# Strassen for the down matmuls of two token pairs in the second MoE, with weight forms kept in DRAM

## Chip, cores and metric

One core of a Trainium2 chip runs the kernel. The metric is the device time in microseconds (us); the time given for a kernel is the median of its runs. Matrix products run on TensorE (PE), elementwise work on VectorE (DVE), ScalarE (ACT) and GpSimd (POOL), and all DMAs named here are issued in order by SyncE (SP).

## What is computed

```python
attn = np.exp(scores); attn = attn / (np.sum(attn, axis=-1, keepdims=True) + 1e-09)
x = np.matmul(attn, v)                        # 4 batches, 8 heads, 576 positions, 64 wide
x = x as [2304 tokens, 512]
xn = x / np.sqrt(np.mean(x * x, axis=-1, keepdims=True) + 1e-06) * rms_g
g = xn @ w_gate
x = silu(g) * (xn @ w_val) @ w_out            # first MoE: 512 -> 1536 -> 512
h = x @ w_in                                  # second MoE: 512 -> 2048
out = (h - np.tanh(h)) @ w_out2               #             2048 -> 512
```

## The kernel before

The 2304 tokens are cut into 6 blocks of 384. Attention runs over 20 query tiles, interleaved with the first MoE, block by block; then the second MoE runs alone. Each matmul with a weight is done in three parts: weight and activation are both split into an fp16 high and an fp16 low half, and `mm3` (L692) adds high·high, high·low and low·high, each a 128x128 by 128x384 matmul. The results of the first MoE go to DRAM (`x2d`, L734) and come back as `x2f`, 768 KB a block (`x2_load`, L1089).

The weights of the second MoE arrive as float64 words. `w2_tasks` is a list of small steps that the loops call in between the matmuls of the first MoE's last blocks and of the first block of the second MoE. A piece is loaded (512 KB, L557), decoded to fp32 by three DVE operations (`decode`, L559 to L561), squared and summed on ACT (L250), and after a power-of-two scale is known it is split in place into halves by ACT (L575) and DVE (L576). The weights then stay in SBUF in `WI` (512 -> 2048) and `W2` (2048 -> 512) to the end.

In the second MoE, blocks 0 and 1 are plain: `up2` (L1245) makes one 128-row slice of the 2048 hidden rows from 12 matmuls, 16 slices a block, and `down2` (L1260) one 128-row slice of the output from 48 matmuls, 4 a block. So a plain block has 192 matmuls up and 192 down. Blocks 2/3 and 4/5 go up as pairs by Strassen (Winograd's form): `pair_up` (L1274) makes 7 products instead of 8 for each of eight slices `s8`, each product being 2 x `mm3` = 6 matmuls, 336 matmuls a pair instead of 384. It needs sums of weight quarters (S1, S2, S4 in a tile `SF`, S3 in place of a quarter of `WI`, made by `form_tasks`, L1182 and L1181) and sums of the activations (`x2_forms`, L1126). Each product has its own PSUM bank; DVE adds them (L1302), ACT and DVE apply h − tanh h and split the result into halves (L1288 to L1291). The down half of the pairs is plain.

Order of the work: the Tile framework places each engine's instructions in one fixed list and adds the waits. An engine takes its list in order, so an instruction that waits holds up all behind it on that engine, and on SP all DMAs behind it.

## Time and profile before

| | |
|---|---|
| median of 3 runs | 1067.97 us (1066.99 to 1068.27) |
| the profiled execution, first to last instruction (span) | 1066.9 us |
| TensorE busy | 971.0 us, 91% of the span, mean granted clock 0.979 |
| VectorE busy | 680.1 us, 64% |
| ScalarE busy | 606.2 us, 57% |
| GpSimd busy | 325.6 us, 31% |
| DMA | 76.81 MB, mean 72 GB/s |

The profiled execution has no other time of its own than its span; it stands 1.1 us under the median. A matmul's row gives its start and a modelled duration of some 0.33 us, of which half lies under the next one; "idle before" is what the engine waited just before a row, and the name behind `<-` is what ended the wait. The stage windows divide the span at chosen times; PEclk is the clock that TensorE was granted as a share of full speed (1.00 is 2.4 GHz, 0.50 is 1.2 GHz).

### The profile page before, as it was taken

Reading aid. Unit: us, or ns where it says so; the run is one execution under the profiler, and the core shown is the slowest. Engines: PE = TensorE matmul, PEld = TensorE weight load, DVE = VectorE, ACT = ScalarE, POOL = GpSimd, SP = SyncE. Lnnn points to the kernel's source line nnn. Section 1 sums busy time; section 2 is a strip of 40 time slices with the busy share of each in tenths; the row PEclk is TensorE's granted clock in tenths of the full one; section 3 lists DMA queues with packets and bytes.
Section 4 is the critical chain, followed back from the end, with each engine's and each line's share of the span. In section 5 each row is a group of like instructions: output and inputs, shape, how many; then the busy total and the mean of one; then the engine's idle time right before and its main releaser. Section 6 shows DMA issues by size and latency. Waiting matters only on the chain.

```text
span 1066.9 us, 19296 instructions
## 1 busy us (share of the span) xinstructions
PE 971.0 (91%) x7471; PEld 616.9 (58%) x7472; DVE 680.1 (64%) x1472; ACT 606.2 (57%) x1172; POOL 325.6 (31%) x405
## 2 busy tenths in 40 slices
PE   1488967798899999999999899999999999999998
PEld 1377645455566666666667555655666666666664
DVE  8986998975585641674553878579792683438500
ACT  6589657776665763776766446446571462225400
POOL 5121275423462541364356112100200251015200
PEclk9986989999999999999999999999999999999999
DMA  8614524241211112210100960131102000000000
GB/s 269 257 36 108 191 72 144 65 132 38 64 27 53 25 44 74 77 28 21 54 19 11 309 233 1 46 135 68 60 1 82 8 2 16 23 23 1 8 23 30
DMA packets 49439, 76.81 MB, mean 72 GB/s; under 512 B 25891, under 2 KB 35203, under 8 KB 48835
## 3 DMA queue, kind: packets, MB, share of 16 engines
q1 hardware_dynamic: 49346, 75.58, 22.7%
q8 instruction: 58, 0.95, 0.4%
q14 instruction: 35, 0.28, 0.1%
...
## 4 chain that ended last, share of the span: by engine, by line
PE 63%; DVE 15%; DMA 9%; ACT 6%; issue 4%; POOL 2%; SPq 1%; ACTq 0%; DVEq 0%; POOLq 0%
PE m L693 11%; PE m L695 11%; PE m L694 11%; PE mm L693 7%; PE mm L695 7%; PE mm L694 7%; DVE w L560 1%; PE pv L494 1%; PE st L452 1%; PE st L453 1%; DMA wo<-wv 1%; DMA raw<-wo 1%; DMA w<-wo 1%; DVE w L559 1%; DMA qst<-qa 1%
## 5 line engine op out<-in xcount | busy, mean ns | idle before, releaser
L693 PE MATMUL mm<-xth,w 128*128 128x384 f16 x480 | 158.0, 329 | 28.2 <-DVE tm L712 20.9
L694 PE MATMUL mm<-xtl,w 128*128 128x384 f16 x480 | 157.9, 329 | 0.6 <-DMA xtl<-xl 0.6
L695 PE MATMUL mm<-xth,w 128*128 128x384 f16 x480 | 157.5, 329 | 0.1
L694 PEld LDWEIGHTS <-w 128*128 128x128 f16 x960 | 94.4, 98 | 87.1 <-issue 32.7
L693 PEld LDWEIGHTS <-w 128*128 128x128 f16 x960 | 94.9, 99 | 62.7 <-ACT w L575 3.7
L695 PEld LDWEIGHTS <-w 128*128 128x128 f16 x960 | 94.2, 98 | 63.5 <-issue 2.5
L693 PE MATMUL m<-dh,w 128*128 128x384 f16 x384 | 124.0, 326 | 0.7 <-ACT t L1271 0.7
L694 PE MATMUL m<-dl,w 128*128 128x384 f16 x384 | 124.4, 326 | 0.0
L695 PE MATMUL m<-dh,w 128*128 128x384 f16 x384 | 124.0, 326 | 0.0
L474 POOL TENSOR_TENSOR phl<-pf,phl 128x512 f16<-128x512 f32 (+2 forms) x90 | 97.8, 1094 | 40.1 <-ACT phl L467 38.7
L724 POOL TENSOR_TENSOR sl<-tm,sh 128x384 f16<-128x384 f32 x72 | 74.8, 1039 | 112.9 <-ACT sh L723 105.6
L462 POOL TENSOR_SCALAR_AFFINE_SELECT pf<-pf 128x128 f32<-128x128 f32 (+3 forms) x105 | 46.9, 449 | 175.0 <-ACT pf L460 174.7
L1263 POOL TENSOR_SCALAR io<-iso,isd 128x1 f32<-128x1 f32 x24 | 12.0, 501 | 258.8 <-ACT t L1271 258.8
L460 ACT ACTIVATE pf<-st,lnp,ilam 128x512 f32<-128x512 f32 (+2 forms) x105 | 73.0, 703 | 23.0 <-PE st L453 17.9
L1271 ACT ACTIVATE t<-m,io 128x384 f32<-128x384 f32 x24 | 13.8, 578 | 126.1 <-PE m L695 123.0
L693 PE MATMUL mm<-sh,wo 128*128 128x384 f16 x240 | 77.9, 326 | 2.3 <-DVE tm L712 2.3
L695 PE MATMUL mm<-sh,wo 128*128 128x384 f16 x240 | 78.1, 326 | 0.5 <-DVE wo L576 0.5
L694 PE MATMUL mm<-sl,wo 128*128 128x384 f16 x240 | 78.1, 326 | 0.0
L452 PE MATMUL st<-q,kl 128*128 128x128 f16 (+1 forms) x456 | 62.9, 217 | 8.6 <-DVE q L368 2.7
L1302 DVE SCALAR_TENSOR_TENSOR c<-m,sigma,c 128x768 f32<-128x768 f32 x32 | 32.5, 1015 | 57.3 <-PE m L695 55.6
L1291 POOL TENSOR_TENSOR dl<-c,dh 128x768 f16<-128x768 f32 x28 | 48.0, 1731 | 54.9 <-ACT dh L1290 54.9
L712 DVE SCALAR_TENSOR_TENSOR tm<-tm,mm 128x384 f32<-128x384 f32 x60 | 32.8, 547 | 43.9 <-ACT tm L711 41.4
...
## 6 DMA issues: line engine op xcount, KB each, us to landing
...
```

Of the source, the lines that this page charges most:

```text
L452: P.matmul(out=ps[:, o:o + w], lhsT=K2[sl][:, ks], rhs=q2_of(T)[:, h, 0:w], start=True, stop=False)
L460: A.activation(out=pf[:, 0:o], in_=ps[:, 0:o], func=ACTF.Exp, scale=bstate[b]["ilam"][:, hh:hh + 1], bias=lnp)
L462: G.affine_select(out=dg, in_=dg, pattern=[[0, len(heads)], [1, w]], compare_op=ALU.is_ge, fill=0.0, base=0, channel_multiplier=-1)
L474: G.tensor_tensor(out=u["pl"][:, 0:n], in0=u["pf"][:, 0:n], in1=u["ph"][:, 0:n], op=ALU.subtract)
L693: P.matmul(out=ps, lhsT=wh, rhs=xh, start=first, stop=False)
L694: P.matmul(out=ps, lhsT=wh, rhs=xl, start=False, stop=False)
L695: P.matmul(out=ps, lhsT=wl, rhs=xh, start=False, stop=last)
L712: V.scalar_tensor_tensor(out=t, in0=t, scalar=1.0, in1=ps, op0=ALU.add, op1=ALU.mult)
L724: moe_pend.append(lambda: G.tensor_tensor(out=SH["l"][:, f, :], in0=t, in1=SH["h"][:, f, :], op=ALU.subtract))
L1271: A.activation(out=t, in_=ps, func=ACTF.Copy, scale=io)
L1291: by.tensor_tensor(out=DL[:, s8, ds, :], in0=c[:, ds], in1=DH[:, s8, ds, :], op=ALU.subtract)
L1302: V.scalar_tensor_tensor(out=out, in0=ps, scalar=sg, in1=c0, op0=ALU.mult, op1=ALU.add)
```

## The change

The down half of the two pairs becomes Strassen as well (`pair_down`): 7 products for each of two 128-row slices `e`, each of 8 x `mm3` = 24 matmuls, so 336 matmuls a pair in place of 384. It needs the hidden activations in seven forms. Three of them (`HL`) are made in `pair_up` by `gated`; four are sums that `g_forms` makes from fp32 copies `CR`: three DVE subtractions, one ACT copy to fp16 of 4 x 384 columns, and the low halves on DVE and POOL. Two of the eight `g_forms` run inside `pair_up` (`EARLY`), six in the first three products of `pair_down`.

Both sets of weights need seven forms, which no longer fit in SBUF beside the rest. So each decoded fp32 piece is written to DRAM (`pk_d`, 32 of 256 KB), `sum_tasks` reads the pieces back (32 loads of 256 KB) while blocks 0 and 1 run, makes S1 to S4 from them on POOL and DVE, splits them (`put`), and writes all forms to DRAM as fp16 halves (`wi_d`, `wo_d`, 56 writes of 256 KB). `pair_up` then reads its weights from a ring of three buffers `wr`, one load of 128 x 7168 B (896 KB) for each `s8`, 16 in all; `pair_down` from a ring of three buffers `wd`, one load of 1 MB for each product, 14 in all. The load for a slot is issued when the last matmul that reads it is done.

PSUM: M1, M6, M7 and M4 of a slice accumulate in one bank (`ps_a`, 2 of them) and M5, M3 in another (`ps_d`, 2). Between two of those products ACT copies the partial sum out (`keep`), so the next product into that bank waits for ACT. The SBUF pool of `WI` and `W2` is closed before the pairs, and its place in the pool stack has changed.

```diff
+    pk_d = [dram.tile([128, 512], FP32, name=f"pk{i}") for i in range(32)]
+    wi_d = [dram.tile([4, 128, 7, 2, 256], FP16, name=f"wid{i}") for i in range(2)]
+    wo_d = [dram.tile([128, 2, 8, 256], FP16, name=f"wod{i}") for i in range(7)]
...
-    def mm3(ps, wh, wl, xh, xl, k, first, last):
-        P.matmul(out=ps, lhsT=wh, rhs=xh, start=first, stop=False)
-        P.matmul(out=ps, lhsT=wh, rhs=xl, start=False, stop=False)
-        P.matmul(out=ps, lhsT=wl, rhs=xh, start=False, stop=last)
+    def mm3(ps, wh, wl, xh, xl, k, first, last, free=False):
+        P.matmul(out=ps, lhsT=wh, rhs=xh, start=first, stop=False, skip_group_check=free)
+        P.matmul(out=ps, lhsT=wh, rhs=xl, start=False, stop=False, skip_group_check=free)
+        P.matmul(out=ps, lhsT=wl, rhs=xh, start=False, stop=last, skip_group_check=free)
...
+    def put(to, t, s):
+        t4 = t.rearrange("p (c w) -> p c w", c=4)
+        A.activation(out=to[:, :, 0, :], in_=t4, func=ACTF.Copy, scale=s)
+        V.scalar_tensor_tensor(out=to[:, :, 1, :], in0=t4, scalar=s, in1=to[:, :, 0, :], op0=ALU.mult, op1=ALU.subtract)
+    def keep_form(i, g, k, q, t):
+        if i == 0:
+            SY.dma_start(out=wi_d[g][:, :, q, k].rearrange("c p w -> p c w"), in_=t.rearrange("p c h w -> p c (h w)"))
+        else:
+            SY.dma_start(out=wo_d[q][:, g, 4 * k:4 * k + 4], in_=t.rearrange("p c h w -> p c (h w)"))
...
+            sq_accum(slot_f(W, n), tl[i, g % 2][:, n % 8:n % 8 + 1], junk16(raw))
+            SY.dma_start(out=pk_d[16 * i + 4 * g + k], in_=slot_f(W, n))
...
+            put(slot4(W, n), slot_f(W, n), sc[i][:, g % 2:g % 2 + 1])
+            q = {(0, 0): A11, (0, 1): A12, (1, 1): A22}.get((g // 2, k // 2))
+            if q is not None:
+                keep_form(i, g % 2, k % 2, q, slot4(W, n))
...
+    def sum_tasks(in_p, fo_p):
+        tasks = []
+        d = {}
+        def load(i, g, k):
+            for nm, gg, kk in (("a21", g + 2, k), ("a22", g + 2, k + 2), ("a11", g, k), ("a12", g, k + 2)):
+                d[nm] = in_p.tile([128, 512], FP32, name=nm, tag=nm)
+                SY.dma_start(out=d[nm], in_=pk_d[16 * i + 4 * gg + kk])
+        def form(i, g, k, q, t):
+            fo = fo_p.tile([128, 4, 2, 128], FP16, name="fo", tag="fo")
+            put(fo, t, sc[i][:, g:g + 1])
+            keep_form(i, g, k, q, fo)
+        def first(i, g, k):
+            d["t"] = in_p.tile([128, 512], FP32, name="sft", tag="sft")
+            G.tensor_tensor(out=d["t"], in0=d["a21"], in1=d["a22"], op=ALU.add)
+            G.tensor_tensor(out=d["a21"], in0=d["a11"], in1=d["a21"], op=ALU.subtract)
+        def second(i, g, k):
+            form(i, g, k, S1, d["t"])
+            form(i, g, k, S3, d["a21"])
+        def third(i, g, k):
+            V.tensor_tensor(out=d["t"], in0=d["t"], in1=d["a11"], op=ALU.subtract)
+            form(i, g, k, S2, d["t"])
+            V.tensor_tensor(out=d["a12"], in0=d["a12"], in1=d["t"], op=ALU.subtract)
+            form(i, g, k, S4, d["a12"])
+        for i in range(2):
+            for g in range(2):
+                for k in range(2):
+                    for f in (load, first, second, third):
+                        tasks.append(lambda i=i, g=g, k=k, f=f: f(i, g, k))
+        return tasks
...
-        def three(g, k):
-            t, w, v = (place(i) for i in (2 * k, 2 * k + 1, 4))
...
+    def load_up(n):
+        if n < 16:
+            wr[n] = wr_p.tile([128, 7, 2, 256], FP16, name="wr", tag="wr")
+            SY.dma_start(out=wr[n], in_=wi_d[n % 8 // 4][n % 4])
+    D_ORDER = (0, 2, 1, 3)
+    for f in range(16):
+        up2(0, f)
+        run_tasks(w2t, -(-(nt - n5) // 14))
+    run_tasks(w2t, 1000)
+    st_ws.close()
...
+    for d in D_ORDER:
+        down2(0, d)
+        run_tasks(sums, 2)
+    for f in range(16):
+        up2(1, f)
+        if f < 14:
+            run_tasks(sums, 1)
+        if f == 7:
+            x2_stat(2)
+    x2_forms(2)
+    for n in range(3):
+        load_up(n)
+    for d in D_ORDER:
+        down2(1, d)
+        run_tasks(sums, 3)
+    for st in (st_sf, st_a, st_d, st_pm):
+        st.close()
+    ps_a = pool(st_m2, "ps_a", bufs=2, space=PSUM)
+    ps_d = pool(st_m2, "ps_d", bufs=2, space=PSUM)
+    wd_p = pool(st_m2, "wd", bufs=3, side="right")
+    c_p = pool(st_m2, "cr", bufs=1)
+    t2_p = pool(st_m2, "t2", bufs=2)
+    CR = c_p.tile([128, 9, 4, TB], FP32, name="cr")
+    HL = c_p.tile([128, 8, 3, 2, TB], FP16, name="hl")
...
+        def product(ps, s8, q, form, start):
+            w = wr[8 * p + s8]
             for k in range(2):
-                h, l = wf["of"](q, g, k)
-                mm3(ps[:, 0:TB], h[:, o], l[:, o], xf[:, form, 0, k, :], xf[:, form, 1, k, :], k, k == 0, k == 1)
...
+        def keep(s8, nm):
+            t = t2_p.tile([128, TB], FP32, name=nm, tag=nm)
+            A.activation(out=t, in_=st[s8]["a"], func=ACTF.Copy, scale=sg(s8))
+            st[s8][nm] = t
+        def add(s8, i, ps, nm):
+            V.scalar_tensor_tensor(out=st[s8]["c"][:, i], in0=ps, scalar=sg(s8), in1=st[s8][nm], op0=ALU.mult, op1=ALU.add)
+        def m1(s8):
+            st[s8] = dict(a=bank(ps_a, "pa"), c=CR[:, c_at(p, s8)])
+            product(st[s8]["a"], s8, A11, B11, True)
+            keep(s8, "s1")
+        def m2(s8):
+            f = bank(ps_mm, "mm")
+            product(f, s8, A12, B21, True)
+            add(s8, 0, f, "s1")
+        def m6(s8):
+            product(st[s8]["a"], s8, S2, T2, False)
+            keep(s8, "u2")
+        def m5(s8):
+            st[s8]["d"] = bank(ps_d, "pd")
+            product(st[s8]["d"], s8, S1, T1, True)
+        def m7(s8):
+            product(st[s8]["a"], s8, S3, T3, False)
+            keep(s8, "u3")
+            add(s8, 3, st[s8]["d"], "u3")
+        def m4(s8):
+            product(st[s8]["a"], s8, A22, T4, False)
+            A.activation(out=st[s8]["c"][:, 2], in_=st[s8]["a"], func=ACTF.Copy, scale=sg(s8))
+        def m3(s8):
+            product(st[s8]["d"], s8, S4, B22, False)
+            add(s8, 1, st[s8]["d"], "u2")
...
+            A.activation(out=HL[:, s8, hs, 0, :], in_=c[:, hc], func=ACTF.Copy)
+            (V if s8 == 7 else G).tensor_tensor(out=HL[:, s8, hs, 1, :], in0=c[:, hc], in1=HL[:, s8, hs, 0, :], op=ALU.subtract)
...
         for s8 in range(8):
-            product(m1, "11", B11, s8)
-            A.activation(out=s1[:, 0], in_=m1[:, 0:TB], func=ACTF.Copy, scale=sg)
-            product(m26[:, 0], "12", B21, s8)
-            product(m26[:, 1], "S2", T2, s8)
-            add(c[:, 0:2], m26[:, :, 0:TB], s1.to_broadcast([128, 2, TB]))
-            product(m7, "S3", T3, s8)
-            add(c[:, 2], m7[:, 0:TB], c[:, 1])
-            product(m5, "S1", T1, s8)
-            add(c[:, 1:4:2], m5[:, 0:TB].unsqueeze(1).to_broadcast([128, 2, TB]), c[:, 1:3])
-            product(m34[:, 0], "S4", B22, s8)
-            product(m34[:, 1], "22", T4, s8)
-            rest(c, s8, 0, 3, V if s8 == 7 else G)
-            add(c[:, 1:3], m34[:, :, 0:TB], c[:, 1:3])
-            rest(c, s8, 1, 1, V if s8 == 7 else G)
+            m6(s8)
+            m5(s8)
+            if s8 < 7:
+                m1(s8 + 1)
+            m7(s8)
+            gated(s8, slice(0, 4, 3), slice(0, 2), slice(0, 4, 3))
+            if s8 < 7:
+                m2(s8 + 1)
+            m4(s8)
+            m3(s8)
+            gated(s8, slice(1, 3), 2, 2)
+            load_up(8 * p + s8 + 3)
+            if s8 in EARLY:
+                g_forms(p, EARLY.index(s8))
+            if j == 2 and s8 == 4:
+                x2_stat(4)
+    EARLY = (3, 5)
...
+    def c_at(p, s8):
+        return (9 - p + s8) % 9
+    def g_form(p, s8):
+        return CR[:, (8 - p + s8) % 9].rearrange("p a t -> p (a t)").bitcast(FP16).rearrange("p (f l t) -> p f l t", f=4, l=2)
+    def g_forms(p, s8):
+        c = CR[:, c_at(p, s8)]
+        V.tensor_tensor(out=c[:, 0:2], in0=c[:, 1:4:2], in1=c[:, 0:2], op=ALU.subtract)
+        V.tensor_tensor(out=c[:, 3], in0=c[:, 3], in1=c[:, 0], op=ALU.subtract)
+        V.tensor_tensor(out=c[:, 2], in0=c[:, 2], in1=c[:, 3], op=ALU.subtract)
+        t = g_form(p, s8)
+        A.activation(out=t[:, :, 0, :], in_=c, func=ACTF.Copy)
+        for e, fs in ((V, slice(0, 2)), (G, slice(2, 4))):
+            e.tensor_tensor(out=t[:, fs, 1, :], in0=c[:, fs], in1=t[:, fs, 0, :], op=ALU.subtract)
+    DOWN = [(A11, "h", 0), (A12, "h", 2), (S4, "h", 1), (S2, "t", 3), (S3, "t", 1), (S1, "t", 0), (A22, "t", 2)]
+    def load_down(n):
+        if n < 14:
+            wd[n] = wd_p.tile([128, 2, 8, 256], FP16, name="wd", tag="wd")
+            SY.dma_start(out=wd[n], in_=wo_d[DOWN[n % 7][0]])
...
+        for i, (q, kind, f) in enumerate(DOWN):
+            w = wd[7 * p + i]
+            for e in range(2):
+                s = st[e]
+                if q == A11:
+                    s["a"] = bank(ps_a, "pa")
+                if q == S1:
+                    s["d"] = bank(ps_d, "pd")
+                ps = s["a"] if q in (A11, S2, S3, A22) else s["d"] if q == S1 else bank(ps_mm, "mm")
+                for s8 in range(8):
+                    v = HL[:, s8, f] if kind == "h" else g_form(p, s8)[:, f]
+                    mm3(ps, w[:, e, s8, 0:128], w[:, e, s8, 128:256], v[:, 0, :], v[:, 1, :], s8, s8 == 0 and q not in (S2, S3, A22), s8 == 7, True)
+                if q == A11:
+                    s["s1"] = keep(ps, e, "s1")
+                elif q == A12:
+                    total(j, e, ps, s["s1"])
+                elif q == S4:
+                    s["m3"] = keep(ps, e, "m3")
+                elif q == S2:
+                    s["u2"] = keep(ps, e, "u2")
+                    V.tensor_tensor(out=s["m3"], in0=s["m3"], in1=s["u2"], op=ALU.add)
+                elif q == S3:
+                    s["u3"] = keep(ps, e, "u3")
+                elif q == S1:
+                    total(j + 1, e, ps, s["m3"])
+                    total(j + 1, e + 2, ps, s["u3"])
+                else:
+                    t = out_tile()
+                    A.activation(out=t, in_=ps, func=ACTF.Copy, scale=io[:, e:e + 1])
+                    send(j, e + 2, t)
+            if i < 3:
+                with newest() if i == 0 else ExitStack():
+                    for s8 in range(2 + 2 * i, 4 + 2 * i):
+                        g_forms(p, s8)
+            load_down(7 * p + i + 3)
+            if i == 3 and j == 2:
+                with newest():
+                    x2_forms(4)
+    run_tasks(sums, 1000)
+    for n in range(3):
+        load_down(n)
+    for j in (2, 4):
+        if j == 2:
+            x2_load(4)
+            x2_load(5)
+        pair_up(j)
+        pair_down(j)
```

The change moves instructions at three places. First, **SP around the first loads of the second MoE's weights** (`w<-win`, while block 4 of the first MoE runs); `xth`/`xtl` are the transposed activations of the first MoE's last block. Before:

```order
L557 DMA w2_8286<-win 128x1024 x11
L547 DMA_TRANSPOSE xth_7255<-xh_8015 128x4x128
L557 DMA w2_8286<-win 128x1024
L548 DMA_TRANSPOSE xtl_7256<-xl_8016 128x4x128
L557 DMA w2_8286<-win 128x1024 x2
```

Now:

```order
L1116 DMA x2f_8793<-x2d_115 128x1536
L537 DMA_TRANSPOSE xth_7296<-xh_8056 128x4x128
L538 DMA_TRANSPOSE xtl_7297<-xl_8057 128x4x128
L547 DMA w2_8339<-win 128x1024 x8
L1042 DMA pk0_116<-wi_8338 128x512
L547 DMA w2_8339<-win 128x1024
L1042 DMA pk1_117<-wi_8338 128x512
```

The loads now stand behind the two transposes, and from the ninth on each stands behind a write of a decoded piece.

Second, **DVE in the same stretch**. `wi<-w2` rows are decodes (three a piece), `tm<-tm,mm` rows are the first MoE's own gate and value work, which frees PSUM banks for PE. Before:

```order
L561 SCALAR_TENSOR_TENSOR wi_8285<-w2_8286,wi_8285 128x512
L544 SCALAR_TENSOR_TENSOR ss_8014<-ss_8014 128x1
L712 SCALAR_TENSOR_TENSOR tm_8060<-tm_8060,mm_8046 128x384
L559 TENSOR_SCALAR wi_8285<-w2_8286 128x512
L543 TENSOR_SCALAR ss_8014<-ss_8014 128x1
L722 SCALAR_TENSOR_TENSOR tm_8060<-tm_8060,mm_8063 128x384
L559 TENSOR_SCALAR wi_8285<-w2_8286 128x512
```

Now:

```order
L702 SCALAR_TENSOR_TENSOR tm_8101<-tm_8101,mm_8087 128x384
L536 SCALAR_TENSOR_TENSOR xl_8057<-x_7881,ss_8055,xh_8056 128x512
L712 SCALAR_TENSOR_TENSOR tm_8101<-tm_8101,mm_8104 128x384
L702 SCALAR_TENSOR_TENSOR tm_8133<-tm_8133,mm_8119 128x384
L712 SCALAR_TENSOR_TENSOR tm_8133<-tm_8133,mm_8136 128x384
L549 TENSOR_SCALAR wi_8338<-w2_8339 128x512
L550 SCALAR_TENSOR_TENSOR wi_8338<-w2_8339,wi_8338 128x512
L551 SCALAR_TENSOR_TENSOR wi_8338<-w2_8339,wi_8338 128x512
```

All of block 4's own DVE work now comes ahead of the first decode; the decodes follow in one run of 15 pieces before block 5's first `tm` row.

Third, **PE in `pair_up` around the first reuse of a ring slot**. `pa` and `pd` are the accumulating banks, `wr` the ring's buffers; the rows are the last matmul of M3 of slice 0, the first of the four products behind it (6 matmuls each), and the first matmul of M1 of slice 3. Now:

```order
L685 MATMUL pd_10635<-xf_9173,wr_10278 128x384
L683 MATMUL pa_10642<-xf_9173,wr_10280 128x384
...
L683 MATMUL pd_10702<-xf_9173,wr_10280 128x384
...
L683 MATMUL pa_10709<-xf_9173,wr_10282 128x384
...
L683 MATMUL pd_10769<-xf_9173,wr_10282 128x384
...
L683 MATMUL pa_10776<-xf_9173,wr_10692 128x384
```

SP at the same place. Now:

```order
L1398 DMA wd_10604<-wod6_156 128x4096
L1247 DMA wr_10692<-wid0_148 128x3584
L1247 DMA wr_10759<-wid1_149 128x3584
L1247 DMA wr_10826<-wid1_149 128x3584
L1247 DMA wr_10893<-wid1_149 128x3584
```

Buffer `wr_10692` takes the slot of `wr_10278`, so its load can start only behind the first of these PE rows, and the last PE row waits for it: four products, 24 matmuls, lie between. The slices run in pairs, so the same pattern comes back at slices 5 and 7, and three times in the second pair: six places. At the other slices more than ten products lie between.

## Rows read from the trace of the kernel before

**Rows 1.** Windows by stage: start:end us, length, busy us (xcount) by engine, PEclk, DMA share, GB/s.

```profile
600.00:640.00 40.00, 39.42 (x242) 23.63 (x242) 33.58 (x64) 19.70 (x51) 5.56 (x3) 1.00 0.81 259
715.00:730.00 15.00, 12.20 (x74) 7.11 (x73) 14.28 (x30) 10.31 (x23) 0.00 (x0) 1.00 0.41 134
730.00:760.00 30.00, 30.00 (x187) 18.21 (x186) 29.76 (x62) 19.64 (x34) 5.75 (x2) 1.00 0.21 66
840.00:880.00 40.00, 40.00 (x248) 24.09 (x247) 35.45 (x38) 25.32 (x33) 21.27 (x12) 1.00 0.00 1
```

**Rows 2.** Timeline, second MoE's first and last matmul and what follows: start us, us, instruction.

```profile
699.02 0.33 PE L693 MATMUL m<-x2f,wi 128*128 128x384 f16 x1
...
1063.15 0.33 PE L695 MATMUL m<-dh,w 128*128 128x384 f16 x1
...
1063.56 0.58 ACT L1271 ACTIVATE t<-m,io 128x384 f32<-128x384 f32 x1 [8.10 <-PE m L695]
```

**Rows 3.** Waits of PE from 560 us on: us in total, times, longest.

```profile
PE mm L693 <- DVE tm L712: 2.9, 2, 1.4
PE m L693 <- DVE tm L712: 2.8, 2, 2.4
PE m L693 <- DVE t L1256: 2.5, 3, 1.2
PE m L693 <- ACT t L1271: 0.7, 1, 0.7
```

**Rows 4.** Timeline of PE: three rows behind a wait, [idle before <-releaser].

```profile
594.46 0.32 PE L693 MATMUL mm<-xth,w 128*128 128x384 f16 x1 [1.44 <-DVE tm L712]
...
599.96 0.32 PE L693 MATMUL mm<-sh,wo 128*128 128x384 f16 x1 [1.44 <-DVE tm L712]
...
642.20 0.32 PE L693 MATMUL m<-xth,w 128*128 128x384 f16 x1 [2.42 <-DVE tm L712]
```

**Rows 5.** Windows of 1 us behind the longest of these waits.

```profile
643.00:644.00 1.00, 1.00 (x5) 0.46 (x3) 1.00 (x4) 1.00 (x4) 0.00 (x0) 0.50 0.00 0
646.00:647.00 1.00, 1.00 (x7) 0.57 (x6) 0.74 (x1) 0.59 (x2) 0.56 (x1) 0.83 0.09 16
```

**Rows 6.** Timeline of DVE: the first decode of the second MoE's weights.

```profile
591.94 0.43 DVE L559 TENSOR_SCALAR wi<-w 128x512 int32<-128x512 int32 x1 [1.71 <-DMA w<-win]
```

**Rows 7.** Groups of DVE from 560 to 720 us: busy us, mean ns of one.

```profile
L560 DVE SCALAR_TENSOR_TENSOR wi<-w,wi 128x512 int32<-128x512 int32 x16 | 10.9, 685 | 0.0
```

**Rows 8.** Groups from 730 us to the end, shapes apart.

```profile
L1291 POOL TENSOR_TENSOR dl<-c,dh 128x768 f16<-128x768 f32 x28 | 48.0, 1731 | 54.9 <-ACT dh L1290 54.9
L1288 ACT ACTIVATE ta<-c,isd 128x768 f32<-128x768 f32 x32 | 29.8, 932 | 29.9 <-DVE c L1302 29.9
L1290 ACT ACTIVATE dh<-c 128x768 f16<-128x768 f32 x32 | 26.8, 840 | 8.7 <-DVE c L1289 8.6
L1305 ACT ACTIVATE c<-mm,sigma 128x384 f32<-128x384 f32 x16 | 9.2, 576 | 7.1 <-PE mm L695 7.1
L1133 ACT ACTIVATE xf<-x2f 128x1536 f16<-128x1536 f32 x4 | 5.9, 1479 | 3.9 <-DMA x2f<-x2d 3.2 <-DVE sf L1182 0.7
```

**Rows 9.** Timeline of SP: issue of one 768 KB load.

```profile
734.39 0.33 SPq L1091 DMA_DIRECT2D x2f<-x2d  x1
```

**Rows 10.** Windows over that load's data.

```profile
736.50:737.00 0.50, 0.50 (x6) 0.30 (x4) 0.50 (x3) 0.50 (x2) 0.00 (x0) 1.00 0.99 393
737.50:738.00 0.50, 0.50 (x5) 0.31 (x4) 0.50 (x2) 0.08 (x1) 0.00 (x0) 1.00 0.74 307
738.00:738.50 0.50, 0.50 (x5) 0.30 (x4) 0.50 (x2) 0.00 (x0) 0.00 (x0) 1.00 0.01 0
```

**Rows 11.** Timeline of SP and ACT: a 768 KB load between two writes, and its reader.

```profile
753.93 0.34 SPq L1272 DMA_DIRECT2D out<-t  x1
754.32 0.43 SPq L1091 DMA_DIRECT2D x2f<-x2d  x1
...
760.59 1.48 ACT L1133 ACTIVATE xf<-x2f 128x1536 f16<-128x1536 f32 x1 [3.24 <-DMA x2f<-x2d]
```

More of the change, by code (lines that the diff above doesn't have):

```diff
@@ L105, in tile_forget_attention_moe_moe2 @@
     wide = [None]
-    half = []
-    pairs = [bool(0)]
-    def mm_pair():
-        half.clear()
-        return wide[0].tile([128, 2, 512], FP32, name="m2", tag="m2", bufs=2)
     def mm_tile():
-        if wide[0] is not None and not pairs[0]:
+        if wide[0] is not None:
             return wide[0].tile([128, 512], FP32, name="m2", tag="m2", bufs=4)[:, 0:TB]
-        if pairs[0]:
-            if not half:
-                pair = mm_pair()
-                half.extend(pair[:, i, 0:TB] for i in range(2))
-            return half.pop(0)
         return ps_mm.tile([128, 512], FP32, name="mm", tag="mm")[:, 0:TB]
@@ new lines, in tile_forget_attention_moe_moe2, with p2 @@
+    sc = [small(const, [128, 2], FP32, f"sc2{i}") for i in range(2)]
+    simin, sig = small(const, [128, 1], FP32, "simin"), small(const, [128, 2], FP32, "sigma")
+    def p2(src, e, sg):
+        V.tensor_scalar(out=e, in0=src.bitcast(I32), scalar1=24, scalar2=None, op0=ALU.logical_shift_right)
+        V.tensor_scalar(out=e, in0=e, scalar1=37.0, scalar2=50.0, op0=ALU.max, op1=ALU.add)
+        V.tensor_scalar(out=e, in0=e, scalar1=23, scalar2=None, op0=ALU.logical_shift_left)
+        V.reciprocal(out=sg, in_=e.bitcast(FP32))
@@ new lines, in w2_tasks @@
+        for i in range(2):
+            for g in range(2):
+                for gg in (g, g + 2):
+                    for k in range(4):
+                        tasks.append(lambda i=i, gg=gg, k=k: piece(i, gg, k))
+                tasks.append(lambda i=i, g=g: chain(i, g))
+                for gg in (g, g + 2):
+                    for k in range(4):
+                        tasks.append(lambda i=i, gg=gg, k=k: conv(i, gg, k))
+            if i == 0:
+                tasks.append(last)
+                n_in = len(tasks)
@@ L1086, in tile_forget_attention_moe_moe2 @@
     x2s = {}
-    XF = [None]
     def x2_load(j):
@@ L1353, in tile_forget_attention_moe_moe2 @@
+    run_tasks(sums, 1000)
[7 more added lines that the diff above has]
+        pair_down(j)
+    for st in (st_m2, st_w2):
         st.close()
```

292 lines of the change are left out of this document (104 added, 188 removed).

## Prediction

> **What bounds the kernel now.** I read the windows by stage first, then the waits of PE in the second half, then the timeline around each wait. From 730 us to the end PE is busy in every stage, as in the stretches at 730 and at 840 us, at full clock [rows 1]. So the second MoE is bound by the number of its matmuls, and a matmul less is worth its spacing. That comes from the first and the last matmul of the second MoE, 699.02 and 1063.15 us [rows 2]. Between them lie 4 x 192 plain up, 2 x 336 Strassen up and 4 x 192 plain down, 2208 in all, and some 3.8 us of waits (the two rows for the second MoE give 3.2 [rows 3], a wait too short for a row of its own here another 0.6). (1063.15 − 699.02 − 3.8) / 2207 = 0.163 us. The half-overlapped 0.33 us of a row is not the cost.
>
> PE's other stalls from 560 us on lie in the end of the first MoE: 2.9 and 2.8 us behind DVE's `tm`, two each [rows 3]. DVE is the busier helper there: 33.58 of 40 us from 600 to 640, and 14.28 of 15 from 715 to 730, where PE has 12.20 [rows 1]. It decodes the second MoE's weights in the same list.
>
> **The change, part by part.** All sums are against the profiled span of 1066.9 us; the median of the runs is 1.1 us above it, which I add at the end.
>
> *Removed matmuls.* The down of a pair falls from 384 to 336; 2 x 48 = 96 x 0.163 = **−15.6 us**. All of them lie on the path.
>
> *First decodes.* Before, the first decode sits in DVE's list ahead of block 4's `tm`, and waits for its load until 591.94 after 1.71 us idle [rows 6]. PE then stands 1.44 us twice, at 594.46 and 599.96, for `tm` [rows 4]. Now all of block 4's `tm` rows come ahead of the first decode. **−2.9 us**; bounds −2.9 and 0.
>
> *Later decodes.* The price is that decoding starts some 8 us later (the loads stand behind two transposes), near 600 us. A decode row takes 0.685 us [rows 7]; with its two companions a piece takes about 1.5, so the 15 pieces ahead of block 5's first `tm` end near 624 us. PE has 144 down matmuls of block 4 and block 5's first ones in between, and needs that bank near 628. So I expect no new wait there, and little of the old ones in block 5: 2.8 us in waits [rows 3], of which 2.42 stand at 642.20 [rows 4], and behind that one the granted clock is half, 0.50 (1.2 GHz), for three windows of 1 us and 0.83 in a fourth [rows 5], which loses 3 x 0.5 + 0.17 = 1.7 us. At stake are 4.5 us. DVE is still full, so I take **−3 us**; bounds −4.5 and +2 (15 decodes end 6 us late).
>
> *Plain up of block 0.* The wait for DVE's `t` is 2.5 us [rows 3]. Fewer pieces fall into it, but the writes and form splits add some. **−2 us**; bounds −3 and +2.
>
> *Forming the sums.* 8 rounds, each four loads, two POOL operations, two DVE subtractions, four splits on ACT and DVE and four writes, in down 0, up 1 and down 1: 576 matmuls or 94 us, 11.7 us a round, and 7.8 in up 1, where a round takes four slices of 12 matmuls. On SP the loads stand in one line behind the writes and the outputs. PE's list in down 1 mixes slices of the output, so a late step is seldom waited for. **+2 us** for this and for the handover of pools to the pairs; bounds 0 and 8.
>
> *The rings in `pair_up`.* This is the change's new wait. Between the last matmul that reads a buffer and the first that needs its reload lie 24 matmuls, 24 x 0.163 = 3.9 us, at six places; elsewhere ten products or more. No load of 896 KB into a busy kernel is in the trace. Lower bound: a lone 768 KB load is issued at 734.39 [rows 9], runs at up to 393 GB/s, and its data has ended within the window that closes at 738.00 [rows 10], 3.6 us; scaled by size only the data part of 2 us grows, by 0.3, so 3.9: no wait. Upper bound: the load issued at 754.32 beside two writes of 192 KB lets its reader start at 760.59, 6.27 us [rows 11]; 6.6 for 896 KB, 2.7 us late, six times 16. The ring's loads have SP and the DMA engines nearly alone, as the lone one has, so I take 4.6 us with the release and landing, 0.7 late at each, **+4 us**; bounds 0 and 16, and more if the clock falls in the waits.
>
> A rule bears on this. The Trainium skill, "DMA: Bandwidth & Descriptors", section Bandwidth, lists 6.15 us for a 1 MB load; an estimate from it for 896 KB is 5.4 us, six waits of 1.5 us, and the sum would be 5 us higher. The trace is at odds with it: its lone 768 KB load is done in 3.6 us from issue to the last data [rows 9, 10].
>
> *ACT in `pair_up`.* The copies of partial sums sit between products of one bank. For each slice ACT does four copies of 384 columns at 0.576, two tanh at 0.932, copies of 768 (0.840) and 384 columns (0.576) [rows 8]: 5.6 us; PE has 42 matmuls, 6.8 us. Two slices with one early form add 1.48 (the 1536-column row): 12.7 of 13.7. ACT fits, without much slack; **+2 us** for short waits, bounds 0 and 6.
>
> *Forms in `pair_down`.* Six forms, each ACT 1.48 and then POOL 1.73 [rows 8], 19.3 us end to end, while the first three products give PE 3 x 48 x 0.163 = 23.5 us. The cover is there; without it the first S2 product waits up to 4 us a pair. **0**; bounds 0 and 8. The `wd` loads have 7.8 us or more of matmuls each. **0**.
>
> *End.* As before: the last matmul, an ACT copy at 1063.56 [rows 2], a write. **0**.
>
> Sum: −15.6 − 2.9 − 3 − 2 + 2 + 4 + 2 = −15.5, a span of 1051.4, against the median **1052.5 us**. A measurement of this kernel can tell about 0.2%, 2.1 us, from no change; so faster means under 1065.8, slower above 1070.1.
>
> **Rivals.**
>
> *The rings come late (slower).* If a reload takes 7.5 us instead of 4.6, the wait is 3.6 at six places, 22 us; and if the clock falls behind each, as it did behind 2.42 us [rows 5], 1.7 more each, 10 us. The sum without the ring is 1048.5; the time would be 1070 to 1080. It decides at a wait of 3.2 us a place (or 1.5 with the clock). For it: the load that took 6.27 us to its reader. Against it: that one ran beside two others. I give a middle case, waits of 1.5 to 2.5 us, 1058 to 1064, 0.12, and the slow end 0.09.
>
> *Everything is hidden.* The ring waits for nothing, and the stalls of block 5 and of up 0 all go: −15.6 − 2.9 − 4.5 − 2.5 = 1041.4 span; with a little left over 1043 to 1047. For it: PE has been kept full through every stretch from 730 us on. Chance 0.15.
>
> *The helpers bind between 600 and 800 us.* DVE was at 29.76 of 30 from 730 us [rows 1], and now it also splits sums and waits in line for SP's loads; block 5 and block 0 stall as before and block 1 stalls for 5 us more: 1057 to 1062. For it: DVE's share; against it: POOL, with nothing to do from 715 to 730 us and 5.75 of 30 after that [rows 1], takes half of the sums' additions. Chance 0.15.
>
> *The change does less than it says.* The forms of `pair_down` come late at both pairs, 8 us each: 1066 to 1070, no change. PE would stand before the first S2 product. Chance 0.05.
>
> **How the numbers follow.** The forecast itself (1047 to 1057) gets 0.44, the hidden case 0.15, helpers 0.15, middle ring 0.12, late forms 0.05, slow ring 0.09. Range 1044 to 1062: it leaves out the late forms, the slow ring, the lower part of the hidden case and the upper part of the middle ring. Faster 0.44 + 0.15 + 0.15 + 0.12 = 0.86; same 0.05; slower 0.09.
>
> **What would show it.** PE has 96 matmuls fewer. No wait of PE for `tm` between 590 and 605 us, and less than 2 us in block 5. In each `pair_up`, PE waits for a DMA into `wr` at three places, 0.5 to 1 us each, and nowhere else for a DMA. Waits of PE for ACT copies sum to about 2 us. None for POOL in `pair_down`. The granted clock stays 1.00 from 700 us on. The prediction is wrong if PE waits for `wr` over 2 us a place, if the clock is at half in `pair_up`, or if the stretch from the last product of block 1 to the first of `pair_up` has a hole of over 3 us.

## The result and the profile after

The changed kernel takes 1073.99 us (median of 5 runs, 1072.48 to 1077.85) against 1068.2 us before: ratio 1.0053, 95% interval 1.0037 to 1.007. It is slower by half a percent, where 1052.5 us and faster were forecast; the time lies outside the range. The profiled execution spans 1074.3 us, 7.4 us more than before; its time of 1075.98 us stands 2.0 us above the median.

The page, part 1 (busy us, share of the span and instructions of each engine):

```profile
PE 964.1 (90%) x7372; PEld 607.1 (57%) x7372; DVE 726.7 (68%) x1518; ACT 660.7 (62%) x1256; POOL 370.8 (35%) x421
```

TensorE has 99 records fewer (96 are the removed matmuls, and the scales of the weights need 4 records fewer; a record is missing here or there), and yet a lower share than the 91% of before, while all four other engines have more to do. The waits of PE from 560 us on, total us, times and longest, to be held against [rows 3]:

```profile
PE mm L683 <- DVE t L1413: 4.0, 2, 2.0
PE pa L683 <- DMA wr<-wid: 3.3, 5, 0.8
PE m L683 <- DVE t L1226: 3.0, 4, 1.4
PE mm L684 <- DVE xf L1170: 2.9, 1, 2.9
PE pa L683 <- ACT u L1304: 2.8, 3, 1.3
PE mm L683 <- DVE tm L702: 1.8, 1, 1.8
PE pd L683 <- DVE cr L1308: 1.7, 2, 0.9
PE m L683 <- DVE x2e L121: 1.5, 1, 1.5
PE m L683 <- ACT t L1239: 1.5, 1, 1.5
PE pa L684 <- POOL cr L1391: 1.1, 2, 0.6
PE mm L683 <- DVE cr L1308: 1.1, 1, 1.1
PE pa L683 <- ACT cr L1389: 0.5, 1, 0.5
PE m L683 <- DVE tm L702: 0.3, 1, 0.3
```

Before, this list had the four kinds of [rows 3] and one more of 0.6 us, 9.5 us together; now it has thirteen and 25.5. The windows by stage tell where they lie (columns as in [rows 1]):

```profile
760.00:780.00 20.00, 16.63 (x101) 9.82 (x100) 12.15 (x18) 9.91 (x18) 4.55 (x5) 1.00 0.77 262
780.00:800.00 20.00, 14.37 (x82) 7.93 (x80) 19.33 (x37) 15.34 (x26) 4.17 (x3) 0.96 0.63 197
900.00:920.00 20.00, 17.98 (x111) 10.74 (x110) 14.50 (x21) 8.21 (x11) 6.61 (x3) 1.00 0.54 193
1020.00:1040.00 20.00, 17.98 (x101) 10.27 (x100) 13.80 (x20) 7.81 (x9) 6.66 (x4) 0.91 0.36 125
```

Before, PE was busy all through both stretches from 730 us on in [rows 1], and its one wait there was 0.72 us at 1055.51 us. The first and the last matmul of the second MoE:

```profile
695.36 0.33 PE L683 MATMUL m<-x2f,wi 128*128 128x384 f16 x1
...
1070.53 0.33 PE L685 MATMUL pa<-cr,wd 128*128 128x384 f16 x1
```

The second MoE's part, from its first matmul to the end of the span, is 1074.3 − 695.36 = 378.9 us; before it was 1066.9 − 699.02 = 367.9 [rows 2]. So it grew by 11.0 us although 15.6 us of matmuls left it. In what follows "part" means this stretch, and it is used to compare profiles: its start lies anywhere between 690.2 and 697.3 us in the profiles of the kernels below, whose first 560 us hold the same program.

A wait costs more than the idle time in its row: behind 2.02 us idle the matmuls start 911.27 − 908.92 = 2.35 us apart instead of 0.16 (rows below), 0.17 more than the idle time. For a list of waits I add 0.16 each.

### The profile page after: what moved, and what is told of

It reads as the page before. It is cut to its first block, busy times and chain, and to the rows that moved or that the text cites. A ratio compares the mean times of both kernels' runs of the same rounds, so it can differ in the third digit from the quotient of the medians.

```text
span 1074.3 us, 19602 instructions
## 1 busy us (share of the span) xinstructions
PE 964.1 (90%) x7372; PEld 607.1 (57%) x7372; DVE 726.7 (68%) x1518; ACT 660.7 (62%) x1256; POOL 370.8 (35%) x421
## 4 chain that ended last, share of the span: by engine, by line
PE 44%; DVE 23%; DMA 11%; issue 8%; ACT 7%; POOL 5%; SPq 1%; POOLq 0%; ACTq 0%; DVEq 0%
PE mm L683 8%; PE mm L685 7%; PE mm L684 7%; POOL cr L1391 3%; PE m L683 2%; PE m L685 2%; PE m L684 2%; PE pa L684 2%; PE pa L683 2%; PE pa L685 2%; PE pv L484 2%; PE st L442 1%; DMA wr<-wid 1%; DVE w L550 1%; PE st L443 1%
## 5 line engine op out<-in xcount | busy, mean ns | idle before, releaser
L683 PE MATMUL mm<-xth,w 128*128 128x384 f16 x480 | 160.4, 334 | 25.2 <-DVE tm L702 16.5
L685 PE MATMUL mm<-xth,w 128*128 128x384 f16 x480 | 159.6, 334 | 0.0
L464 POOL TENSOR_TENSOR phl<-pf,phl 128x512 f16<-128x512 f32 (+2 forms) x90 | 94.8, 1061 | 40.4 <-ACT phl L457 38.0
L684 PEld LDWEIGHTS <-w 128*128 128x128 f16 x704 | 69.7, 99 | 65.2 <-issue 27.9
L685 PEld LDWEIGHTS <-w 128*128 128x128 f16 x704 | 69.7, 99 | 47.7 <-issue 3.7
L683 PEld LDWEIGHTS <-w 128*128 128x128 f16 x704 | 70.0, 99 | 46.9 <-ACT w L565 3.7
L1347 POOL TENSOR_TENSOR hl<-cr,hl 128x768 f16<-128x768 f32 (+1 forms) x28 | 41.9, 1501 | 105.4 <-ACT hl L1346 105.4
L443 PE MATMUL st<-qc,kc 128*128 128x128 f16 (+1 forms) x456 | 59.1, 216 | 0.6 <-DMA qc<-rt 0.6
L457 ACT ACTIVATE phl<-pf 128x512 f16<-128x512 f32 (+2 forms) x90 | 49.4, 558 | 11.9 <-POOL pf L452 6.2
L713 ACT ACTIVATE sh<-tm 128x384 f16<-128x384 f32 x72 | 37.1, 517 | 29.0 <-DVE tm L712 28.7
L1391 POOL TENSOR_TENSOR cr<-cr 128x768 f16<-128x768 f32 x16 | 37.7, 2354 | 45.2 <-ACT cr L1389 45.2
L442 PEld LDWEIGHTS <-kl 128*128 128x128 f16 x480 | 45.1, 103 | 13.4 <-DVE kl L288 7.8
L486 PE MATMUL pv<-vt,phl 128*128 128x65 f16 (+1 forms) x360 | 49.7, 196 | 2.2 <-ACT phl L457 1.5
```

The costliest lines, as they stand in the source:

```text
L442: P.matmul(out=ps[:, o:o + w], lhsT=K2[sl][:, ks], rhs=q2_of(T)[:, h, 0:w], start=True, stop=False)
L443: P.matmul(out=ps[:, o:o + w], lhsT=KC[sl][:, ks], rhs=qc_of(T)[:, h, 0:w], start=False, stop=True)
L457: A.activation(out=ph[:, 0:o], in_=pf[:, 0:o], func=ACTF.Copy)
L464: G.tensor_tensor(out=u["pl"][:, 0:n], in0=u["pf"][:, 0:n], in1=u["ph"][:, 0:n], op=ALU.subtract)
L486: P.matmul(out=ps[0:w, o:o + 65], lhsT=u["ph"][:, cs], rhs=vs[:, 64:129], start=(c == 0), stop=False)
L683: P.matmul(out=ps, lhsT=wh, rhs=xh, start=first, stop=False, skip_group_check=free)
```

## The experiments

### What holds up PE between 760 and 800 us

Seven waits lie there, 8.9 us idle, 10.0 with the 0.16 each, and the half clock behind the last of them, 1.7 us more. Ahead of them stands one long gap on ACT. SP's issues, then ACT and PE in the changed kernel:

```profile
753.91 0.84 SPq L1247 DMA_DIRECT2D wr<-wid  x2
754.85 0.40 SPq L1024 DMA_DIRECT2D wid<-fo  x1
755.98 0.99 SPq L1247 DMA_DIRECT2D wr<-wid  x1
...
756.20 0.56 ACT L1239 ACTIVATE t<-m,io 128x384 f32<-128x384 f32 x1
764.28 0.72 ACT L1019 ACTIVATE fo<-a,sc 128x512 f16<-128x512 f32 x1 [7.52 <-DMA wid<-fo]
...
765.52 0.32 PE L683 MATMUL m<-xf,wi 128*128 128x384 f16 x1 [1.48 <-ACT t L1239]
```

The scheduler has put the first three loads of the ring, 2.75 MB, ahead of or between the form writes, at 753.91 and 755.98 us. ACT's next form copy waits 7.52 us for a form buffer, that is for a write which stands in the same DMA queues; behind it in ACT's list stand the output copy that PE waits for and all tanh rows of up 1. That was my first theory (A); the rival (B) was that the work on the sums holds up up 1 however the loads come.

**e1_late_wr** spreads the three loads (`after_sp` holds a load behind SP's newest instruction):

```diff
+        if f in (9, 12, 15):
+            with after_sp():
+                load_up((f - 9) // 3)
     x2_forms(2)
-    for n in range(3):
-        load_up(n)
```

> The three first loads of the ring of pair_up come one by one behind later rows of SP (the first behind four more rounds' rows), instead of all three at 753.9 to 757.0 us. Theory A (the burst): 2.75 MB put into the DMA queues at once made the write of a form buffer last 9 us, so ACT stood 7.52 us for that buffer and everything of up 1 came late. Then ACT's longest wait for a form write falls under 2 us, PE's waits between 760 and 800 us (8.9 us in seven) fall under 4 us, the half clock behind 798 us goes, and the time falls by 6 to 10 us to 1064 to 1068. Rival B (DVE and ACT simply have too much work in up 1 and down 1): the hole of ACT goes, but PE waits over 7 us in that stretch all the same, and the time stays within 3 us of 1074.

Measured: 1076.69 us (ratio to before 1.0085, 1.006 to 1.011), part 381.2 us. ACT's waits for form buffers and sums from 740 to 800 us:

```profile
ACT fo L1019 <- POOL sft L1092: 5.3, 3, 2.8
ACT fo L1019 <- DMA wid<-fo: 2.2, 2, 1.7
```

The gap is gone (1.7 us at most for the write), and PE still waits 10.4 us in six places between 760 and 794 us. A falls: the burst makes the gap, but the gap is not what costs the time.

**e2_fo6** (`"fo", bufs=6` for `bufs=3`) leaves the burst and gives ACT room.

> Six buffers for the forms in sum_tasks instead of three; the three ring loads stay where they are. Theory A: the write in the queue behind the burst is still slow, but ACT has three more buffers to go on with, so its 7.52 us wait falls under 3 us and PE's waits between 760 and 800 us under 5 us; time 1065 to 1070. Rival B (too much work): PE's waits there stay above 7 us. Rival C (the loads of the fp32 pieces stand behind the burst too, so POOL and DVE starve): ACT's wait for the form write goes but one of similar length for POOL's sum comes in its place, and the time stays above 1071.

Measured: 1073.44 us (1.0041, 1.0026 to 1.0055), part 379.1. The gap changed its name, as rival C said:

```profile
ACT fo L1019 <- POOL sft L1092: 11.6, 4, 8.7
```

The longest of these is 8.7 us: the loads of the fp32 pieces stand behind the burst as well. PE's waits there are 7.1 us in four.

**e7_no_sums** takes the sums out (`sums = []`, and `conv` writes the quarters' halves in the places of S1 to S4).

> The weight sums S1 to S4 are not formed: sum_tasks is left out, and the four forms are written to DRAM as copies of the quarters' halves, so the output is not the reference's. The 56 form writes, the rings, the pairs and all their matmuls stay as they are. It measures what forming the sums costs PE. Theory B (the sum steps in the in-order lists of ACT and DVE hold up the tanh work that frees PE's banks): PE's waits between 745 and 800 us, 8.9 us in seven in the changed kernel with a half clock behind the last, fall under 2 us, and the span falls by about 10 us to 1062 to 1066. Theory A (the burst of ring loads alone): the same burst now meets form writes made in block 0, ACT waits for nothing in up 1, and the result would be the same; so this run gives the size, and the late-load run has already told the two apart. Rival D (the waits there come from x2_stat and x2_forms, which are still in): 5 us or more of waits stay.

Measured in one run: span 1062.6, part 366.7 us, 12.2 less than the changed kernel; between 690 and 830 us PE has no wait at all. x2_stat and x2_forms are still in, so rival D falls. This is the size of the largest cost: forming the sums beside blocks 0 and 1 costs PE 12 us.

**e8_spread** (8 steps in up 1 instead of 14, up to 16 in down 1):

```diff
-        if f < 14:
+        if f % 2 == 0:
             run_tasks(sums, 1)
...
-        run_tasks(sums, 3)
+        run_tasks(sums, 4)
```

> Up 1 runs 8 steps of sum_tasks instead of 14 and down 1 up to 16 instead of 12: what only pair_down needs is formed later. Theory B: the PE waits of 8.9 us between 760 and 800 us fall to 3 to 6 us, since fewer steps stand in ACT's and DVE's lists ahead of the tanh rows; time 1066 to 1071. If the sums' steps in up 1 did not matter (Theory A alone), the wait of ACT behind the burst stays at 5 to 8 us and the time within 2 us of 1074.

Measured: 1074.67 us (1.0071, 1.0049 to 1.0093), part 379.5; the same seven waits, 9.6 us. It tells nothing about B: ACT's list is the same row for row, since the scheduler fills its list by what it reckons to be ready, not by where the program calls the steps. In letters (f a form copy of the sums, O an output copy, T a tanh of up 1; all other rows left out), for the changed kernel, this one, and the next:

```
changed    ffffOfffOffffOfOTTfTfTfTfTfTfTfTfTfTfTfTfTfTfTffffOOffOO
e8_spread  ffffOfffOffffOfOTTfTfTfTfTfTfTfTfTfTfTfTfTfTfTffffOOffOO
e10_paced  ffffOfffOfOOTTTTTffTTfTfTTTTTffTTTffOffOfffOfffffOffffff
```

**e10_paced** fixes the places: each step of the sums is held behind the newest row of ACT and DVE, two rounds in up 1, four in down 1.

```diff
-        if f < 14:
-            run_tasks(sums, 1)
+        if f % 2 == 0:
+            with newest():
+                run_tasks(sums, 1)
...
-        run_tasks(sums, 3)
+        with newest():
+            run_tasks(sums, 4)
```

> The steps of sum_tasks are held behind the newest work of ScalarE and VectorE, so that their place in those lists is fixed: two rounds in up 1 (one step for every second slice), four in down 1; six form buffers, and the three ring loads one by one behind SP's newest row. Leaving the sums out took PE's waits between 745 and 800 us from 8.9 us to none and the second MoE's part of the span from 378.9 to 366.7 us, so forming them costs 12 us. Theory B (the sum steps stand in the lists ahead of the tanh rows and wait there for GpSimd and the loads): PE's waits in up 1 fall under 3 us, and the second MoE's part of the span falls to 369 to 374 us. Rival (the work of the sums is too much for the engines wherever it stands): the waits move to down 1 and the start of pair_up, and the part stays above 376 us.

Measured: 1081.34 us (1.0124, 1.011 to 1.0138), part 387.2. Up 1 has no wait left, as B said, but the start of `pair_up` pays more, as the rival said (waits of PE from 690 to 860 us, then POOL's first row of three rounds):

```profile
PE pa L683 <- ACT cr L1347: 7.1, 1, 7.1
PE pa L683 <- ACT t L1239: 4.6, 1, 4.6
```

```profile
813.54 1.26 POOL L1092 TENSOR_TENSOR sft<-a,a 128x512 f32<-128x512 f32 x1 [5.78 <-DMA a<-pk]
823.08 1.26 POOL L1092 TENSOR_TENSOR sft<-a,a 128x512 f32<-128x512 f32 x1 [6.93 <-DMA a<-pk]
835.83 1.26 POOL L1092 TENSOR_TENSOR sft<-a,a 128x512 f32<-128x512 f32 x1 [10.14 <-DMA a<-pk]
```

The round that starts at 813.54 us takes 9.5 us. The rows point to its one set of piece buffers: a load of the next round goes out at 818.56 us, 0.5 us behind a DVE row that read a piece of this one (it ends at 818.09), and POOL starts 4.5 us behind that load. The round behind it takes 12.8 us, and POOL's wait of 10.1 us has a second cause: two loads of `wd`, 1 MB each, were issued ahead of three of that round's pieces, at 824.78 and 826.63 us. The long wait of PE, 7.1 us, is a handover: ACT's row of `cr`, which ends it, starts at 843.95 us, after 2.17 us idle for a form write of the last round (`wod<-fo`). Both theories were half of it: the steps hold up the tanh rows where they stand ahead of them, and eight rounds of some ten us in line are too long to be moved out of the way.

### The ring in `pair_up`

```profile
846.90 2.27 SPq L1247 DMA_DIRECT2D wr<-wid  x2
...
850.45 0.33 PE L685 MATMUL pd<-xf,wr 128*128 128x384 f16 x1
851.54 0.34 PE L683 MATMUL pa<-xf,wr 128*128 128x384 f16 x1 [0.77 <-DMA wr<-wid]
```

The rows are SP's issue of the reload and PE's matmuls around the wait. From the issue at 846.90 to the first matmul with the new weights at 851.54 it is 4.64 us; 4.6 were forecast, five waits of 0.58 to 0.77 us in place of six of 0.7. **e4_ring4** gives the ring a fourth buffer (`bufs=4`, loads four ahead).

> Four buffers in the ring of pair_up instead of three. Theory A: the five waits of PE for the ring (0.58 to 0.77 us each, 3.3 us, with the refill of the pipe behind each 4.1 us) are the reload that takes 4.6 us where 3.9 are covered; with a fourth buffer no reload is waited for, and 3 to 4 us go. The burst ahead of pair_up is one load longer (3.67 MB), so ACT's wait for a form write grows by up to 2.4 us and takes 0 to 3 us of it back: 1070 to 1074. Rival (the DMA engines are too slow for the ring in itself): waits for the ring stay, fewer but longer.

Measured: 1071.14 us (1.0027, 1.0015 to 1.004), part 375.8, 3.1 us less, as theory A said; no wait for `wr` is left.

### `pair_down`

DVE, then PE, at the start of the first `pair_down`:

```profile
906.13 2.68 DVE L1385 TENSOR_TENSOR cr<-cr 128x768 f32<-128x768 f32 x3
908.74 1.48 DVE L1386 TENSOR_TENSOR cr<-cr 128x384 f32<-128x384 f32 x3
910.61 0.60 DVE L1413 SCALAR_TENSOR_TENSOR t<-mm,io,s 128x384 f32<-128x384 f32 x1
...
908.92 0.33 PE L685 MATMUL mm<-hl,wd 128*128 128x384 f16 x1
911.27 0.32 PE L683 MATMUL mm<-hl,wd 128*128 128x384 f16 x1 [2.02 <-DVE t L1413]
```

PE's second product there needs a bank of `ps_mm` that DVE empties at 910.61 us (L1413); ahead of it in DVE's list stand the subtractions of six `g_forms`, from 906.13 us on. **e3_s4_bank** gives the S4 product a bank of `ps_d`, which is free there.

> In pair_down the S4 product takes the banks of the pool ps_d, which are free there, instead of ps_mm. Theory A: PE's 2.02 us in each pair_down is a wait for a bank of ps_mm, which VectorE frees late because the subtractions of g_forms stand ahead of it in its list. Then both waits go, with the half clock behind the second, and about 2 x 2.2 + 1.7 = 6 us at most; but the forms, a chain of ACT and POOL that takes 4.0 us each, then set when S2, S3 and S1 start, so that 2 to 4 us of it come back there: net gain 2 to 4 us, 1070 to 1072. Rival (the wait only covers the wait for the forms): PE waits 2 us a pair more on POOL and ACT behind it, and the time does not change.

Measured: 1074.86 us (1.0051, 1.0035 to 1.0068), part 377.4, 1.5 us less. The time has not changed, as the rival said: the waits of 2.02 us are gone, but PE waits 1.65 us for POOL in each pair, and 0.2 to 0.7 us at five places behind it: the forms are next. They come every 4.0 us (ACT's copies at 915.08 and 919.09; ACT, DVE and POOL in turn):

```profile
915.08 1.48 ACT L1389 ACTIVATE cr<-cr 128x1536 f16<-128x1536 f32 x1 [2.81 <-POOL cr L1391]
...
916.59 0.96 DVE L1391 TENSOR_TENSOR cr<-cr 128x768 f16<-128x768 f32 x1 [3.05 <-ACT cr L1389]
...
916.64 2.42 POOL L1391 TENSOR_TENSOR cr<-cr 128x768 f16<-128x768 f32 x1 [1.59 <-ACT cr L1389]
...
919.09 1.48 ACT L1389 ACTIVATE cr<-cr 128x1536 f16<-128x1536 f32 x1 [2.06 <-POOL cr L1391]
```

DVE and POOL start on two halves of the same work at the same time, DVE takes 0.96 and POOL 2.42 us. **e9_low_s4** puts both halves on DVE, with S4 in `ps_d`:

```diff
-        for e, fs in ((V, slice(0, 2)), (G, slice(2, 4))):
+        for e, fs in ((V, slice(0, 2)), (V, slice(2, 4))):
```

> S4 in the free banks as before, and the low halves of all four forms on VectorE instead of two on GpSimd. A row of 768 columns takes VectorE 0.96 us; beside it GpSimd's took 2.41, where it took 1.65 alone. Theory: the two engines hold each other up, and the chain of a form (ACT 1.48, then the slower of the two low halves 2.41, 4.0 in all) falls to ACT 1.48 and 1.92, 3.5 in all. Then the waits of PE for GpSimd in pair_down (1.65 and 0.69 us) go, and the time falls by 3 to 6 us to 1068 to 1071. Rival: the bound is ACT waiting for the buffer that the form before leaves, whoever makes the halves; then PE's waits only change the engine they name and the time stays within 2 us of 1074.

Measured: 1067.9 us, the same as before (0.9997, 0.9978 to 1.0016), 6 us under the changed kernel; part 373.5, from the slowest of its ten runs. ACT's copies now stand 3.46 us apart (913.71 and 917.17 us), near the 3.5 of the theory. A new wait came instead: PE stands 1.85 and 1.60 us for a load of `wd`, once in each pair. The low halves on DVE without the free bank were not run, so the 6 us belong to the two edits together. The two groups, POOL's of the changed kernel and then DVE's of this one, 880 us to the end:

```profile
L1391 POOL TENSOR_TENSOR cr<-cr 128x768 f16<-128x768 f32 x14 | 33.2, 2372 | 40.7 <-ACT cr L1389 40.7
```

```profile
L1391 DVE TENSOR_TENSOR cr<-cr 128x768 f16<-128x768 f32 x28 | 25.6, 955 | 17.1 <-ACT cr L1389 16.9
```

Twice as many rows on DVE take 25.6 us, less than POOL's half alone did.

### The early forms in `pair_up`

ACT, then PE:

```profile
857.64 1.49 ACT L1389 ACTIVATE cr<-cr 128x1536 f16<-128x1536 f32 x1 [0.97 <-DVE cr L1387]
859.03 1.03 ACT L1304 ACTIVATE u<-pa,sigma 128x384 f32<-128x384 f32 x2
...
859.64 0.32 PE L683 MATMUL pa<-xf,wr 128*128 128x384 f16 x1 [1.10 <-ACT u L1304]
```

The form's copy of 1536 columns waits 0.97 us for DVE's subtractions and takes 1.49; the copy of a partial sum that PE waits for stands behind it. **e6_no_early** (`EARLY = ()`, eight forms in `pair_down`):

> None of the eight forms of a pair is made inside pair_up; pair_down makes all eight. Theory: in pair_up the forms' ACT copy of 1536 columns, which waits for VectorE's subtractions, stands in ACT's list ahead of the copies of partial sums, so PE waits 1.1, 0.9 and 0.4 us in the first pair and 1.3 and 0.9 in the second. Without it those five waits go (4.5 us, 5.3 with the refills), and pair_down gets two forms of 4.0 us more to wait for, 4 to 8 us a pair: span 1077 to 1085. Rival (x2_stat or the matmuls' own pace causes them): the waits for ACT and VectorE in pair_up stay.

Measured in one run: span 1085.7, part 392.8 us. The five waits in `pair_up` are gone, and `pair_down` lost some 9.5 us a pair, more than the 4 to 8 expected. The early forms are worth their waits.

### Together

**e11_ring4_low_s4** is e4 and e9 in one.

> Four ring buffers in pair_up, S4 in the free banks and all low halves of the forms on VectorE, the sums as in the changed kernel. The effects lie at different places, so they should add: 3 us for the ring, 6 for the last two together, 9 in all: 1064 to 1067, against 1074 of the changed kernel and 1067.5 to 1068.4 of the kernel before. If VectorE becomes the bound in pair_up (its waits for cr rose where the ring no longer waited), the gain is 6 or less and the time 1067 to 1070.

Measured: 1060.66 us (1057.97 to 1062.38), ratio to before 0.9929 (0.9916 to 0.9943): faster than both kernels, and 13 us under the changed one where 9 were expected. The part is 366.9, 12.0 us under the changed kernel's, where e4 and e9 had 3.1 and 5.4. PE's 3.4 us of waits for `wd`, which were in e9, are gone here, and they are about the rest; why the load comes in time here was not tried. What PE still waits for, the three largest from 690 us on:

```profile
PE m L683 <- DVE t L1226: 3.0, 4, 1.4
PE mm L684 <- DVE xf L1170: 2.5, 1, 2.5
PE m L683 <- ACT t L1239: 1.8, 1, 1.8
```

**e12_all** adds the paced sums, **e13_paced12** the same with three rounds in up 1 (`if f < 12`, and 3 steps for each output slice in down 1).

> The version before this one with the paced sums as well (three form buffers). If theory B holds and the effects add, 9 us for pair_up and pair_down and 5 to 10 us for the sums: 1055 to 1063, faster than the kernel before by 0.5 to 1.2%. If the sums' work is too much wherever it stands, 1064 to 1070.

> As the version with everything, but three rounds of the sums in up 1 (one step behind each of the first 12 slices) and up to three in down 1. With two rounds up 1 had no wait of PE at all and the start of pair_up 13 to 17 us of waits, since four rounds did not fit beside down 1; with the order left to the scheduler up 1 had 7 to 9 us and the start of pair_up 1. If a round costs some 8 us of its chain wherever it stands, three in 31 us of up 1 and two or three in 31 us of down 1 fit nearly, and the waits in both places together fall under 6 us: part of the second MoE 360 to 365 us, time 1053 to 1060. Rival (ScalarE's and VectorE's tanh work leaves no room for a third round in up 1): waits of 6 us or more come back there and the time is 1060 to 1066.

Measured: 1066.85 us (0.9993, 0.9982 to 1.0004) and 1063.17 us (0.9939, 0.992 to 0.9957). Neither beats e11, and both times fell into the range of the rival, though in e13 up 1 waits only 3.9 us, and the start of `pair_up` 5.4. Pacing moves the rounds' cost, it does not remove it. A second set of buffers for the pieces was not tried, so that the one set of buffers makes a round this long is read from the rows and not shown by a run.

## Why the prediction was wrong, point by point

The forecast span was 1051.4 us, the measured one 1074.3.

- *Removed matmuls, −15.6*: right. They are gone, and e7 shows a part below that of before in spite of 15 us of other waits.
- *First and later decodes, −5.9*: the waits of [rows 4] and the half clock of [rows 5] are gone, but a new one came. The rows of ACT, then PE:

```profile
593.86 1.48 ACT L1142 ACTIVATE x2f<-x2f 128x1536 f16<-128x1536 f32 x1 [1.77 <-DMA x2f<-x2d]
...
596.62 0.32 PE L683 MATMUL mm<-xth,w 128*128 128x384 f16 x1 [1.77 <-DVE tm L702]
```
  The square of the first `x2f`, moved up in ACT's list, waits 1.77 us for its load, which SP now issues ahead of the transposes; `tm` and PE wait with it. I had listed that load and weighed only what stood behind it on SP. The part starts 3.7 us earlier in the profile, but that understates the gain, since this execution was late before the change began. PE's first matmul behind the last row of attention, before and then now:
```profile
587.50 0.32 PE L693 MATMUL mm<-xth,w 128*128 128x384 f16 x1
```
```profile
589.32 0.32 PE L683 MATMUL mm<-xth,w 128*128 128x384 f16 x1
```
  From there to the second MoE it is 111.5 us before and 106.0 now, so the term came to 5.5 us, 0.4 short, and 1.8 us of the difference between the two spans lie ahead of it.
- *Plain up of block 0, −2*: all of it went, and with it a wait of 0.6 us for DVE's `iso`: 3.0 us idle in four waits, 3.7 in all, 1.7 better than forecast.
- *Forming the sums, +2*: this is the step that failed most. It came to 12 us (e7; 11.7 by the list of waits). I set the rounds against the matmuls beside them, 11.7 us a round and 7.8 in up 1, and worked out neither how long a round takes nor what its rows hold up. A round is a chain that takes 9.5 us and more (e10), and its rows stand in the same lists as the tanh that frees PE's banks. That "a late step is seldom waited for" held for PE's own list, not for ACT's. The handover to the pairs gave 1.2 more (the wait of 1.07 us at 843.79, `mm` behind DVE `cr`; DVE's first row of `cr` had waited for an output write, `out<-t`, until 843.12).
- *The rings, +4*: right in mechanism and size, 3.3 us idle in five waits, 4.1 in all; e4 took 3.1 off. By the Trainium skill's figure ("DMA: Bandwidth & Descriptors", Bandwidth, from a table of loads issued from GpSimd) the wait would have been an estimated 1.5 us each; the trace differs, with 4.64 us from issue to use for 896 KB.
- *ACT in `pair_up`, +2*: 5.3 us in five waits. The sum of ACT's durations was right and it fitted; but the early form's copy waits for DVE first, and a wait in a list counts for all behind it.
- *Forms in `pair_down`, 0*: 8.2 us, the second large miss. POOL's row was priced at 1.73 us from [rows 8], near the 1.64 that such a row takes alone; beside DVE it takes 2.42, so a form takes 4.0 us, not 3.2, and six take 24, no less than the cover of 23.5. And DVE's subtractions, which I left out of the chain, stand ahead of the row that frees a bank (2 x 2.02 us, with a half clock behind the second).
- *Rivals*: the time came out at "slower", but not by the mechanism I gave that side, the late ring. It is the rival of the helpers (1057 to 1062, 0.15) with the late forms on top: two that I had as alternatives came true together, except that block 0 did not stall. Of the signs, two more failed: PE did wait for POOL in `pair_down` (1.1 us in two places), and the granted clock did fall after 700 us, to 0.50.

The misses add up to 9.7 for the sums, 1.2 handover, 3.3 in `pair_up`, 8.2 in `pair_down`, 0.4 for the decodes and the 1.8 that this execution had lost before them, less 1.7 for block 0 and 0.9 for the last wait of [rows 3], which is gone: 22 of the 22.9 us.
